# Transfers given to SyncE in a written order, and float64 conversions tied behind softmax steps, in an attention and two-stage mixture kernel

## The chip, the cores and the metric

The kernel runs on one core of one Trainium2 chip. The metric is device time in microseconds (us) of one execution of the whole program. Lower is better. TensorE (PE in the rows) multiplies and transposes, VectorE (DVE), ScalarE (ACT) and GpSimd (POOL) work on tiles, and SyncE (SP) gives transfers to the core's DMA engines: its queue takes them one after another, and a transfer whose condition isn't met yet holds back all that stand behind it.

## The reference

Three stages follow each other. Attention over 4 x 12 heads of 448 tokens and 64 features, with normalised queries and keys; a gated layer of 768 -> 1536 -> 768 on its 1792 output rows; and a mixture of 8 experts, of which each row takes one.

```python
q_n, k_n = rmsnorm(q, g_q), rmsnorm(k, g_k)
scores = scale * q_n @ k_n.T                       # 448 x 448 for each of 48 heads
attn = softmax(scores)
x = (attn @ v).reshape(1792, 768)
gate = 1 / (1 + exp(-(x @ w_gate)))
x = (gate * (x @ w_val)) @ w_out                   # moe_: 768 -> 1536 -> 768
e_idx = argmax(x @ w_gate2)                        # moe2_: one of 8 experts for each row
out[rows of e] = gate_w * eom * (relu(x @ w1[e]) @ w2[e])
```

## The kernel before

**Attention** runs in 24 pairs of heads, each in 8 slots, 192 slots in all. `attn_slot(n)` writes the scores of slot n+1 on TensorE (lines 364 and 365), the softmax step of slot n on VectorE (line 377: scale by the row and column factors and take the maximum; line 380 negates it) and ScalarE (line 381: exp with the sum), the four transposes of slot n-2 (line 410), and each fourth slot the product with the values (`av`, line 431). Three things go round through memory. The factors of the keys of a pair are copied by VectorE as a small tile `rk` (line 322), written to `rkd` (line 323) and read back broadcast to `rb` (line 324), which line 377 reads. The sums of a pair are copied as `rr` (line 393), written to `rsd` (line 394), and read back twice as `rs` (line 397); `features` multiplies by it (line 438, `xr`), after which the bank of `av` is free. And tokens `tok` (line 233) are squared on GpSimd (line 271) and summed on VectorE (line 272, into `sa`) for the Newton steps of `inv_root` (lines 289 to 292; its work tiles `sa` and `sw` come from the pool `sw`). `qk` (line 251) and `v` (line 241) are the other loads of a pair.

**The gated layer** runs over two halves of the rows, `moe1_steps(0)` and `moe1_steps(1)`: 48 products `up` (line 555, 18 matmuls each) and six rounds of `down` (line 578). Half 0 needs the first 12 pairs alone, and is woven into the slots from slot 101 on; half 1 begins when attention has ended. In half 0 each of 36 weight pieces comes as float64 (`kind == "wide"` in `piece_in`), in two parts: line 93 loads a part to `w` (two buffers), ScalarE (line 99) and VectorE (lines 101, 103, 105) turn it to float32 in `raw`, line 108 writes it to `wf` for half 1, and `piece_split` (lines 121 and 123) makes the two tiles `whi`, `wlo` that the matmuls read. `want(n)` calls for pieces some steps ahead. Half 1 reads `wf` back (line 111) and loads its features `e` from `xs` (line 874), split by lines 877 and 878. **The experts** come last, and draw on the same functions for their weights.

**What sets the order.** The program is traced in the order of the code, and a scheduler, which has a model of each instruction's time, then orders the instructions of every engine by when the model has them ready. That holds for SyncE's transfers as for arithmetic: a load may be moved ahead of slots, and a conversion between the steps of a softmax. A run-time wait can't change it: each engine takes its instructions as they stand. `tc.issue_after(ins)` ties what is traced under it behind `ins` on that engine's queue, without a wait for its end.

Of the kernel before, what the change touches and what calls it, by code (L numbers as in the profile page):

```python
# [38 lines left out]
PREP = "s1 t2", "K1", "s2", "K2", "", "", "t4", ""  # L39
PAIRED = 64  # L40
# [4 lines left out]
def attn_moe_moe_kernel(ctx, tc, qk, tokqk, tokv, g, wup, wout, wr, w1, w2, out):  # L45
# [34 lines left out]

    def add(key, kind, src, lead=False):
        index[key] = len(pieces)
        pieces.append((kind, src, lead))

    def piece_in(n):
# [4 lines left out]
        if kind == "wide":  # L90
            for c in range(0, DM, DM // PARTS):
                d = mp["w64"].tile([128, DM // PARTS, 2], I32, tag="w64", name="w64")
                last_in[0] = nc.sync.dma_start(
                    out=d, in_=src[:, 2 * c:2 * (c + DM // PARTS)].rearrange("p (c w) -> p c w", w=2))
# [12 lines left out]
            if not lead:  # L107
                nc.sync.dma_start(out=wf[n][:, LG:WO], in_=t[:, LG:WO])
        elif kind == "again":
            c = 0 if lead else LG  # L110
            nc.sync.dma_start(out=t[:, c:], in_=wf[src][:, c:])
        else:
            nc.sync.dma_start(out=t[:, LG:WO], in_=src())
# [82 lines left out]
    lot("sw", 1, 0)  # L196
# [29 lines left out]
    def load_tok(p):  # L226
# [4 lines left out]
        for i in range(0, 16, 8 if p == 0 else 16):  # L231
            i2 = i + 8 if p == 0 else 16
            nc.sync.dma_start(out=t[:, 16 - i2:16 - i], in_=tokqk[b, pr, :, 16 - i2:16 - i])
        tk_t[p] = t

    def load_v(p):
# [4 lines left out]
        nc.sync.dma_start(out=v_, in_=tokv[b, pr])  # L241
        v_t[p] = v_

    def load_qk(p):
# [4 lines left out]
        for h in halves(p):  # L249
            for i in range(2):  # L250
                nc.sync.dma_start(out=t[64 * i:64 * i + 64, :, h], in_=qk[b, pr, :, :, h])
        qk_t[p] = t

    def sums_sq(p):
# [18 lines left out]
        if p > 0:  # L273
            load_tok(p + 1)
# [28 lines left out]
    def krow(p):  # L303
# [4 lines left out]
        if p in DIRECT:  # L308
# [59 lines left out]
    def soft_max(n):  # L368
# [8 lines left out]
        nc.vector.tensor_tensor_reduce(  # L377
# [3 lines left out]
        nc.scalar.activation(  # L381
# [3 lines left out]
    def sums(p):  # L385
# [8 lines left out]
        nc.sync.dma_start(out=rsd[p], in_=rr)  # L394
        t = tile_of("rs", [128, S], F32, "rs")
        for h in range(2):
            nc.sync.dma_start(
                out=t[64 * h:64 * h + 64],
                in_=rsd[p:p + 1, 4 * h:4 * h + 4].rearrange("o c q -> o (c q)").to_broadcast([64, S]))
        rs_t[p] = t  # L400

# [33 lines left out]
    def features(p):  # L435
# [9 lines left out]
        else:  # L445
            nc.sync.dma_start(out=xs[b - 2, pr], in_=t)
# [3 lines left out]
    def stats(p):  # L450
        while did["t"] < p:
            did["t"] += 1
            sums_sq(did["t"])
# [6 lines left out]
    def splits(p):  # L460
        while did["s"] < p:
# [3 lines left out]
            loads(did["s"] + (2 if did["s"] < NPAIR // 2 - 3 else 1))  # L465
# [14 lines left out]
    def attn_slot(n):  # L480
# [7 lines left out]
        if i == 4 and n > 8:  # L488
# [699 lines left out]
```

## Time and profile before

| | us |
|---|---|
| median of 3 runs (lowest, highest) | 1287.24 (1284.73, 1288.29) |
| the profiled execution, its own time | 1288.62 |
| span of that execution, first to last instruction | 1286.8 |
| TensorE busy in it | 1185.8 (92%) |
| VectorE busy | 722.1 (56%) |
| ScalarE busy | 577.1 (45%) |
| GpSimd busy | 382.4 (30%) |

The span falls into stages. Up to 196 us there is attention alone; from 196 to 627 us slots and half 0 are woven; up to 686 us half 0 ends; up to about 952 us half 1; then the experts. A group of rows gives the busy time of each engine in each of these stretches. "Idle before" in a row is the time that the engine stood still just ahead of that instruction, with what ended it. The matmul ends are modelled, and a wait for several things is put down to the one that came last.

### The profile page before, as it was taken

The page shows a single profiled execution, that of the slowest core. Times are in us where ns is not written, and L with a number is a line of the kernel's source. Part 1 is how long each engine was busy: PE and PEld are TensorE (multiplying, and loading weights), DVE is VectorE, ACT ScalarE, POOL GpSimd, SP SyncE. Part 2 cuts the span into 40 slices and gives each one's busy share as a digit, 9 for nine tenths or more (in the row PEclk, how much of TensorE's full clock was granted, in tenths as well). Part 3 has the DMA queues.
Part 4 walks back from the last instruction along what each step waited for, and adds up shares of the span by engine and source line. Part 5 has one row for each costly group of instructions (what it writes and reads, how often), then busy time and mean ns, then how long its engine had stood idle before and what let it go on. Part 6 is the DMA issues. An engine that isn't in the chain of part 4 may idle for free.

```text
span 1286.8 us, 19940 instructions
## 1 busy us (share of the span) xinstructions
PE 1185.8 (92%) x7089; PEld 1039.4 (81%) x7089; DVE 722.1 (56%) x1709; ACT 577.1 (45%) x1174; POOL 382.4 (30%) x318
## 2 busy tenths in 40 slices
PE   5888888999999898997989999999969999999996
PEld 3665657677778787786879999999959998999996
DVE  7877878877568585775754224433454323333342
ACT  4656755556455353543441331122114434555553
POOL 3555645413132031310232000000023434545453
PEclk9888889899999999998999999999998999999999
DMA  9476666656536279476444121121037355566671
GB/s 219 128 181 172 153 163 201 186 144 184 146 96 196 88 199 234 132 197 151 150 139 136 50 63 50 42 71 50 13 123 273 114 194 186 190 207 222 209 269 43
DMA packets 77054, 191.92 MB, mean 149 GB/s; under 512 B 10617, under 2 KB 27513, under 8 KB 76944
## 3 DMA queue, kind: packets, MB, share of 16 engines
q1 hardware_dynamic: 74496, 179.52, 47.8%
q0 software_dynamic: 2448, 11.03, 2.3%
q8 instruction: 58, 0.95, 0.3%
q14 instruction: 52, 0.43, 0.1%
HBM read 154.43 MB, written 36.81 MB: 149 GB/s over the span
## 4 chain that ended last, share of the span: by engine, by line
PE 50%; DMA 2%; DVE 1%; issue 1%; SPq 0%; POOL 0%; ACT 0%; POOLq 0%; DVEq 0%
PE m L555 16%; PE d L1006 10%; PE m L578 9%; PE u L961 7%; PE d L961 3%; PE d L990 2%; DMA w<-in_wup_dram 1%; PE a L431 1%; PE u L940 1%; DMA raw<-in_w_dram 0%; DMA xg<-acc,slot 0%; PE t L410 0%; DMA g<-xg 0%; PE d L998 0%; PE m L597 0%
## 5 line engine op out<-in xcount | busy, mean ns | idle before, releaser
L121 ACT ACTIVATE whi<-raw 128x768 fp32r<-128x768 f32 (+1 forms) x200 | 167.1, 846 | 283.0 <-PE m L555 57.7
L123 POOL TENSOR_TENSOR wlo<-raw,whi 128x768 fp32r<-128x768 f32 (+1 forms) x100 | 188.9, 1896 | 311.4 <-ACT whi L121 268.4
L555 PE MATMUL m<-xh,whi 128*128 128x448 f32 x576 | 215.1, 374 | 4.5 <-DVE tanh L567 3.1
L555 PE MATMUL m<-xl,whi 128*128 128x448 f32 x576 | 212.4, 369 | 0.0
L555 PE MATMUL m<-xh,wlo 128*128 128x448 f32 x576 | 211.1, 367 | 0.0
L123 DVE TENSOR_TENSOR wlo<-raw,whi 128x768 fp32r<-128x768 f32 (+1 forms) x100 | 99.9, 1003 | 187.8 <-ACT whi L121 187.1
L381 ACT ACTIVATE e<-e,m 112x448 f32<-112x448 f32 x192 | 127.4, 665 | 89.8 <-DVE m L380 80.8
L377 DVE CUSTOM_DVE_ANT_0 e<-s,rb,sy 112x448 f32<-112x448 f32 x192 | 127.5, 672 | 32.2 <-PE s L365 17.6
L555 PEld LDWEIGHTS m<-xh,whi 128*128 128x128 f32 x576 | 109.6, 190 | 16.4 <-DVE tanh L567 3.3
L578 PE MATMUL m<-whi,hhi 128*128 128x392 f32 (+1 forms) x336 | 116.7, 352 | 4.5 <-DVE acc L584 2.7
L364 PE MATMUL s<-K,Q 128*112 128x448 f32 x192 | 87.1, 453 | 34.7 <-DVE m L377 24.5
L410 PE MATMUL t<-ident,e 112*112 112x112 f32 x768 | 109.9, 271 | 9.3 <-ACT et L418 6.4
L555 PEld LDWEIGHTS m<-xl,whi 128*128 128x128 f32 x576 | 109.4, 190 | 9.6 <-issue 1.7
L578 PE MATMUL m<-wlo,hhi 128*128 128x392 f32 (+1 forms) x336 | 115.4, 343 | 1.4 <-POOL wlo L123 1.4
L431 PE MATMUL a<-et,v 112*64 112x224 f32 x768 | 109.5, 379 | 7.7 <-ACT et L418 3.8
L410 PEld LDWEIGHTS t<-ident,e 112*112 112x112 f32 x768 | 87.6, 139 | 35.5 <-ACT et L418 8.8
L555 PEld LDWEIGHTS m<-xh,wlo 128*128 128x128 f32 x576 | 109.0, 189 | 8.6
L578 PE MATMUL m<-whi,hlo 128*128 128x392 f32 (+1 forms) x336 | 114.7, 341 | 0.0
L334 POOL TENSOR_TENSOR Q<-qk,Q 64x896 fp32r<-64x896 f32 (+1 forms) x25 | 56.0, 2240 | 172.4 <-DVE Q L333 93.5
L418 ACT ACTIVATE et<-t 112x448 f32<-112x448 f32 x168 | 87.1, 536 | 28.6 <-PE t L410 28.3
L584 DVE TENSOR_TENSOR acc<-m,acc 128x392 f32<-128x392 f32 (+1 forms) x140 | 77.2, 557 | 33.3 <-PE m L578 32.0
L733 POOL DMA_INDIRECT xg<-acc,slot x14 | 14.4, 1028 | 271.0 <-DVE slot L710 267.4
(209 smaller groups left out, 2399.2 us busy)
## 6 DMA issues: line engine op xcount, KB each, us to landing
raw<-in_w_dram SPq DMA_DIRECT2D x128, 384.0 KB
qk<-in_qk_dram SPq DMA_DIRECT2D x46, 448.0 KB
w<-in_wup_dram SPq DMA_DIRECT2D x48, 384.0 KB
tok<-in_tokqk_dram SPq DMA_DIRECT2D x23, 448.0 KB
wf<-raw SPq DMA_DIRECT2D x24, 384.0 KB
w<-in_wout_dram SPq DMA_DIRECT2D x24, 384.0 KB
raw<-wf SPq DMA_DIRECT2D x24, 384.0 KB
rb<-rkd SPq DMA_DIRECT2D x21, 392.0 KB
```

Source lines behind the costliest of these rows:

```text
L121: nc.scalar.activation(out=hi[:, c:], in_=t[:, c:], func=ACTF.Copy)
L123: eng.tensor_tensor(out=lo[:, c:], in0=t[:, c:], in1=hi[:, c:], op=ALU.subtract)
L364: nc.tensor.matmul(ps, lhsT=lhs, rhs=K1_t[p][:, h, :], start=True, stop=False)
L377: nc.vector.tensor_tensor_reduce(out=e, in0=ps, in1=rb_t[p][:, h, :], scale=r_t[p][:, i:i + 1], scalar=-3.0e38, op0=ALU.mult, op1=ALU.max, ...
L381: nc.scalar.activation(out=e, in_=e, func=ACTF.Exp, scale=1.0, bias=m[:, 1:2], accum_out=sum_t[p % 3][:, i, 0:1])
L410: nc.tensor.transpose(ps[0:CH, kc, :], e[:, kc * CH:(kc + 1) * CH], ident[0:CH, 0:CH])
L418: nc.scalar.activation(out=dst, in_=ps[0:CH], func=ACTF.Copy)
L431: nc.tensor.matmul(ps[64 * h:64 * h + 64, hf * 2 * CH:(hf + 1) * 2 * CH], lhsT=v_t[p][:, h, kc, :], rhs=ets[h][:, kc, :], start=(kc == 0), ...
L555: nc.tensor.matmul(ps[:, 0:S], lhsT=a, rhs=x, start=(n == 0), stop=(n == 3 * KD - 1))
L578: nc.tensor.matmul(ps[:, 0:c1 - c0], lhsT=l, rhs=r, start=(i == 0), stop=(i == 5))
L961: nc.tensor.matmul(ps[:, 0:c], lhsT=a, rhs=x[:, k, 0:c], start=(n == 0), stop=(n == 3 * KD - 1))
L1006: nc.tensor.matmul(ps[i, n][0:rows, 0:384], lhsT=l, rhs=s[:, c0:c0 + 384], start=(f == 0 and q == 0), stop=(f == NF2 - 1 and q == 2))
```

## The change

Eight edits, all of which move work and none of which removes an instruction: each engine has as many instructions of each kind as before.

- **A chain on SyncE.** `sp()` issues a transfer tied behind the last one that `sp()` issued. All transfers of attention and of half 0, the loads of `wf` in half 1 and those of `e` go through it, so that SyncE's order is that of the calls. Expert weights and gathers don't.
- **A clock in the code.** `passed(dt)` moves a counter: 1.9 for each slot behind the first pair, and the planner's cost of each step of the gated layer. `later(dt, fn)` puts a call off until the counter has gone dt further. `WAITS` holds four such distances: 1.5 for the small writes (`rkd`, `rsd`, `xs`, the last `wf`), 5.5 for the read-backs `rb` and `rs`, 6.0 for `qk` and `tok`, 5.0 for the `wf` write of a converted piece and the load of the next one.
- **Conversions behind softmax.** The four conversion instructions of each part are tied behind the softmax instructions of the last slot traced, on VectorE (line 377) and ScalarE (line 381).
- **Loads apart from conversions.** `wide_load(n)` loads both parts of a piece, and is called for piece n+1 once piece n has been converted.
- The pool `sw` of `inv_root` gets two buffers in place of one.
- `features` is traced at slot 5 of the next pair in place of 4.
- The first pieces are called for one by one (slots 96, 98 and 100 in place of all at slot 96), and the first `up` is traced at slot 102 in place of 101.
- The zero rows of `xg` stand in the chain in place of behind the last weight load.

```diff
@@ -78,9 +80,55 @@
+    def later(dt, fn):
+        due.append((clock[0] + dt, fn))
+
+    def passed(dt):
+        clock[0] += dt
+        while True:
+            ready = [x for x in due if x[0] <= clock[0]]
...
+            x = min(ready, key=lambda x: x[0])
+            due.remove(x)
+            x[1]()
...
+    def sp(out, in_):
...
+            with tc.issue_after(last_sp[0].ins):
+                last_sp[0] = nc.sync.dma_start(out=out, in_=in_)
...
+    def wide_load(n):
...
+        for c in range(0, DM, DM // PARTS):
+            d = mp["w64"].tile([128, DM // PARTS, 2], I32, tag="w64", name="w64")
+            last_in[0] = sp(
...
+            wide_t[n].append((c, d))
...
     def piece_in(n):
...
         if kind == "wide":
...
+            wide_load(n)
+            after = ExitStack()
+            for x in last_slot.values():
+                after.enter_context(tc.issue_after(x.ins))
+            for c, d in wide_t.pop(n):
...
-            if not lead:
-                nc.sync.dma_start(out=wf[n][:, LG:WO], in_=t[:, LG:WO])
+            after.close()
+
+            def transfers():
+                if not lead:
+                    sp(out=wf[n][:, LG:WO], in_=t[:, LG:WO])
+                wide_load(n + 1)
+
+            later(WAITS[3], transfers)
...
-    lot("sw", 1, 0)
+    lot("sw", 2, 0)
...
-            load_tok(p + 1)
+            if last and clock[0]:
+                later(WAITS[2], lambda: load_tok(p + 1))
+            else:
+                load_tok(p + 1)
...
-        nc.sync.dma_start(out=rkd[p], in_=rr)
-        nc.sync.dma_start(
-            out=t, in_=rkd[p:p + 1].rearrange("o (h c) q -> o h (c q)", h=2).to_broadcast([CH, 2, S]))
+        later(WAITS[0], lambda: sp(out=rkd[p], in_=rr))
+        later(WAITS[1], lambda: sp(
+            out=t, in_=rkd[p:p + 1].rearrange("o (h c) q -> o h (c q)", h=2).to_broadcast([CH, 2, S])))
...
-        nc.sync.dma_start(out=rsd[p], in_=rr)
+        later(WAITS[0], lambda: sp(out=rsd[p], in_=rr))
...
+        later(WAITS[1], back)
...
-            loads(did["s"] + (2 if did["s"] < NPAIR // 2 - 3 else 1))
+            to = did["s"] + (2 if did["s"] < NPAIR // 2 - 3 else 1)
+            if clock[0]:
+                later(WAITS[2], lambda: loads(to))
+            else:
+                loads(to)
...
-        if i == 4 and n > 8:
+        if i == 5 and n > 8:
             features(p - 1)
...
+        passed(1.9 if p > 0 else 0.0)
...
             open_moe()
+            want(0, 0, 0)
+        if n == NSLOT // 2 + 2:
+            want(0, 0, 1)
+        if n == NSLOT // 2 + 4:
             want(0, 1, 2)
...
         fn()
+        passed(c)
```

On SyncE, in attention alone, before (`rkd`, `rb`: write and read-back of the keys' factors; `rsd`, `rs`: of the sums; numbers tell the tiles of one pair from those of the next):

```order
L323 DMA rkd_68<-rk_555 8x112
L233 DMA tok_745<-in_tokqk_dram 112x1024
L324 DMA rb_552<-rkd_68 112x896
L251 DMA qk_899<-in_qk_dram 64x1792
L394 DMA rsd_69<-rr_691 8x112
L251 DMA qk_899<-in_qk_dram 64x1792
L241 DMA v_985<-in_tokv_dram 112x512
L397 DMA rs_694<-rsd_69 64x448 x2
L323 DMA rkd_68<-rk_750 8x112
```

and in the changed kernel, at the same pairs (its line 108 is the one in `sp()`):

```order
L108 DMA rsd_69<-rr_691 8x112
L108 DMA tok_718<-in_tokqk_dram 112x1024
L108 DMA rkd_68<-rk_743 8x112
L108 DMA rs_693<-rsd_69 64x448 x2
L108 DMA qk_785<-in_qk_dram 64x1792 x2
L108 DMA rb_740<-rkd_68 112x896
L108 DMA v_804<-in_tokv_dram 112x512
L108 DMA tok_806<-in_tokqk_dram 112x1024
L108 DMA rsd_69<-rr_886 8x112
```

Most pairs of this stretch now have the same row of transfers: both small writes, `rs`, `qk`, `rb`, `v`, `tok`. Before, `rb` stood right behind its write and one `tok`, and ahead of `qk`.

On SyncE, where slots and half 0 are woven, before (the sums of one pair; `w64` is the load of a part of a piece, `w` in the profile):

```order
L394 DMA rsd_69<-rr_4395 8x112
L397 DMA rs_4398<-rsd_69 64x448 x2
L93 DMA w64_4307<-in_wup_dram 128x768
L323 DMA rkd_68<-rk_4472 8x112
L108 DMA wf_70<-raw_4241 128x768
L93 DMA w64_4313<-in_wup_dram 128x768
L324 DMA rb_4469<-rkd_68 112x896
```

and in the changed kernel, the sums of the same pair:

```order
L108 DMA wf_70<-raw_4267 128x768
L108 DMA w64_4315<-in_wup_dram 128x768
L108 DMA w64_4317<-in_wup_dram 128x768
L108 DMA w64_4341<-in_wup_dram 128x768
L108 DMA w64_4343<-in_wup_dram 128x768
L108 DMA rsd_69<-rr_4377 8x112
L108 DMA wf_70<-raw_4324 128x768
L108 DMA wf_70<-raw_4340 128x768
L108 DMA w64_4445<-in_wout_dram 128x768
L108 DMA w64_4447<-in_wout_dram 128x768
L108 DMA rkd_68<-rk_4441 8x112
L108 DMA rs_4379<-rsd_69 64x448 x2
```

The write of the sums and that of the keys' factors now stand behind loads and write-backs of pieces, with the read-backs together behind them.

On TensorE, at the first `up` (`m` is its bank), before:

```order
L391 MATMUL t<-ident,sum 8x112
L410 MATMUL t<-ident,e 112x112 x4
L320 MATMUL t<-ident,sy 8x112
L431 MATMUL a<-et,v 64x224 x16
L364 MATMUL s<-K_2122,Q 112x448
L365 MATMUL s<-K_2123,Q 112x448
L555 MATMUL m<-xh,whi 128x448
L555 MATMUL m<-xl,whi 128x448
```

and in the changed kernel:

```order
L472 MATMUL t<-ident,e 112x112 x4
L493 MATMUL a<-et,v 64x224 x7
L472 MATMUL t<-ident,e 112x112 x8
L422 MATMUL s<-K_2309,Q 112x448
L423 MATMUL s<-K_2310,Q 112x448
L622 MATMUL m<-xh,whi 128x448
L622 MATMUL m<-xl,whi 128x448
```

Before, 91 scores stand ahead of the first `up`; now there are 103.

## Rows read from the trace of the kernel before

**Rows 1.** Windows: us, busy time (instructions) of PE, PEld, DVE, ACT, POOL; clock; DMA; GB/s.

```profile
10.00:50.00 40.00, 29.27 (x141) 21.58 (x141) 32.41 (x86) 19.36 (x41) 18.05 (x16) 0.91 0.84 196
50.00:196.00 146.00, 121.25 (x816) 86.77 (x816) 114.99 (x345) 97.06 (x240) 81.80 (x96) 0.90 0.63 163
196.00:300.00 104.00, 98.09 (x552) 77.24 (x553) 84.39 (x203) 59.68 (x134) 44.59 (x44) 0.96 0.58 170
300.00:627.00 327.00, 304.41 (x1752) 256.24 (x1749) 224.09 (x546) 157.54 (x342) 69.00 (x45) 0.97 0.59 162
627.00:686.00 59.00, 54.46 (x310) 46.81 (x309) 39.09 (x88) 20.15 (x40) 13.60 (x10) 0.97 0.38 122
686.00:952.00 266.00, 266.00 (x1383) 251.06 (x1382) 102.43 (x180) 62.00 (x100) 9.20 (x10) 1.00 0.19 59
952.00:1287.00 335.00, 311.86 (x2147) 299.45 (x2145) 119.25 (x241) 158.53 (x279) 143.62 (x88) 0.97 0.57 193
```

**Rows 2.** Waits of VectorE, 40 to 300 us: total us, times, longest us.

```profile
DVE e L377 <- DMA rb<-rkd: 10.8, 5, 4.5
...
DVE sa L272 <- POOL sw L290: 6.8, 4, 3.0
DVE xr L438 <- DMA rs<-rsd: 6.1, 5, 2.9
```

**Rows 3.** Waits of TensorE, 40 to 196 us.

```profile
PE s L364 <- DVE m L377: 14.8, 10, 4.2
...
PE a L431 <- DVE xr L438: 2.9, 3, 2.3
```

**Rows 4.** Timeline of SyncE, 57 to 76 us: start, us, transfer, how many.

```profile
63.10 0.43 SPq L323 DMA_DIRECT2D rkd<-rk  x1
63.62 0.33 SPq L233 DMA_DIRECT2D tok<-in_tokqk_dram  x1
69.03 0.31 SPq L324 DMA_DIRECT2D rb<-rkd  x1
```

**Rows 5.** Timeline of VectorE at four moments; idle time before it in brackets.

```profile
72.37 0.68 DVE L377 CUSTOM_DVE_ANT_0 e<-s,rb,sy 112x448 f32<-112x448 f32 x1 [4.47 <-DMA rb<-rkd]
...
114.94 0.62 DVE L438 TENSOR_TENSOR xr<-a,rs 128x448 f32<-128x448 f32 x1 [2.92 <-DMA rs<-rsd]
...
336.81 0.36 DVE L101 TENSOR_SCALAR w<-w 128x384 int32<-128x384 int32 x1 [2.98 <-DMA w<-in_wup_dram]
...
592.82 0.36 DVE L101 TENSOR_SCALAR w<-w 128x384 int32<-128x384 int32 x1 [2.86 <-DMA w<-in_wup_dram]
```

**Rows 6.** Timeline of TensorE at five moments.

```profile
73.12 0.71 PE L364 MATMUL s<-K,Q 128*112 128x448 f32 x1 [4.16 <-DVE m L377]
...
115.62 0.60 PE L431 MATMUL a<-et,v 112*64 112x224 f32 x4 [2.33 <-DVE xr L438]
...
194.94 0.67 PE L364 MATMUL s<-K,Q 128*112 128x448 f32 x1 [2.10 <-DVE m L377]
...
338.26 1.31 PE L431 MATMUL a<-et,v 112*64 112x224 f32 x6 [1.87 <-ACT et L418]
...
593.83 0.42 PE L522 MATMUL m<-tlo,wrs 128*32 128x256 f32 x1 [3.31 <-DVE tlo L514]
```

**Rows 7.** Waits of SyncE, 40 to 300 us.

```profile
SPq L233 <- DVE sa L272: 21.9, 7, 13.0
```

**Rows 8.** Waits of VectorE, 300 to 627 us.

```profile
DVE w L101 <- DMA w<-in_wup_dram: 34.3, 19, 5.3
DVE w L101 <- DMA w<-in_wout_dram: 22.8, 11, 4.3
```

**Rows 9.** Groups of VectorE, 50 to 196 us: count, busy us, mean ns, idle before.

```profile
L377 DVE CUSTOM_DVE_ANT_0 e<-s,rb,sy 112x448 f32<-112x448 f32 x77 | 50.8, 670 | 15.9 <-DMA rb<-rkd 10.8 <-PE s L365 5.0
```

**Rows 10.** Timeline of SyncE where half 0 ends.

```profile
654.95 4.84 SPq L874 DMA_DIRECT2D e<-xs  x5
...
663.20 1.14 SPq L111 DMA_DIRECT2D raw<-wf  x2
```

More of the change, by code (lines that the diff above doesn't have):

```diff
@@ L250, in load_qk, with sums_sq @@
             for i in range(2):
-                nc.sync.dma_start(out=t[64 * i:64 * i + 64, :, h], in_=qk[b, pr, :, :, h])
+                sp(out=t[64 * i:64 * i + 64, :, h], in_=qk[b, pr, :, :, h])
         qk_t[p] = t
-    def sums_sq(p):
+    def sums_sq(p, last=False):
         if p >= NPAIR:
@@ L393, in sums, with back @@
         nc.vector.tensor_copy(out=rr, in_=ps[0:8, 0, :])
-        nc.sync.dma_start(out=rsd[p], in_=rr)
+        later(WAITS[0], lambda: sp(out=rsd[p], in_=rr))
         t = tile_of("rs", [128, S], F32, "rs")
[L396 to L399, printed above, removed]
         rs_t[p] = t
+        def back():
+            for h in range(2):
+                sp(
+                    out=t[64 * h:64 * h + 64],
+                    in_=rsd[p:p + 1, 4 * h:4 * h + 4].rearrange("o c q -> o (c q)").to_broadcast([64, S]))
+        later(WAITS[1], back)
     def transp(n):
@@ L445, in features @@
         else:
-            nc.sync.dma_start(out=xs[b - 2, pr], in_=t)
+            later(WAITS[0], lambda: sp(out=xs[b - 2, pr], in_=t))
     did = {"s": 0, "k": 0, "q": 1, "t": 0}
@@ L541, in lead_put @@
                 out=t[:, 0:LG], in0=ps[:, 32 * j + LG:32 * j + 2 * LG], in1=t[:, 0:LG], op=ALU.add)
-            nc.sync.dma_start(out=wf[n], in_=t)
+            later(WAITS[0], lambda n=n, t=t: sp(out=wf[n], in_=t))
             led.add(n)
@@ L813, in zero_rows @@
             rows = xg[e * NT + r:e * NT + r + n, :]
[L814 to L815 removed]
+            sp(out=rows[:, 0:2 + DM // 4], in_=zrow[0:n])
+            sp(
                 out=rows[:, 2 + DM // 4:].rearrange("p (a c) -> p a c", a=3),
@@ L853, in attn_moe_moe_kernel @@
     first = n
-    left = NSLOT + 5 - first
+    left = NSLOT + 6 - first
     spent = 0.0
@@ L858, in attn_moe_moe_kernel @@
         fn()
+        passed(c)
         spent += c
         while zeroed < NE and spent > total * (0.6 + 0.04 * zeroed):
-            with tc.issue_after(last_in[0].ins):
-                zero_rows(zeroed)
+            zero_rows(zeroed)
             zeroed += 1
-        while n < NSLOT + 5 and (n - first) < left * spent / total:
+        while n < NSLOT + 6 and (n - first) < left * spent / total:
             attn_slot(n)
             n += 1
-    while n < NSLOT + 5:
+    while n < NSLOT + 6:
         attn_slot(n)
         n += 1
+    passed(100.0)
     for tg in range(2):
```

45 lines of the change are left out of this document (29 added, 16 removed).

## The prediction

> **What bounds the kernel now.** I read the stages first [rows 1]. From 686 us to 952 us TensorE is never idle, and from 952 us on the order of all engines is the same in the changed kernel, so whatever the change does to the time it does before 686 us. There TensorE stands still for 24.8 us of attention alone (146.00 less 121.25), 5.9 us up to 300 us, 22.6 us up to 627 us and 4.5 us up to 686 us, and the first 50 us hold some 20 us of start. That is the purse: about 58 us behind the start, of which some belongs to arithmetic.
>
> Attention alone has no single bound: TensorE is busy for 0.83 of it and VectorE for 0.79, at a granted clock of 0.90 of the 2.4 GHz level, and each waits for the other in turn. So a stop of VectorE is a stop of TensorE a moment later. VectorE stops there for memory: 10.8 us for the read-back `rb`, 6.1 us for `rs`, 6.8 us for the Newton work tile [rows 2]. TensorE's waits in the same stretch are mostly for line 377 [rows 3]. The largest pair shows the chain. SyncE writes `rkd` at 63.10 us, gives out a `tok`, and can issue `rb` at 69.03 us alone, when the write has landed [rows 4]. VectorE's next softmax step begins at 72.37 us after 4.47 us of nothing [rows 5], and TensorE's scores at 73.12 us after 4.16 us [rows 6]. Six gaps of TensorE come right behind such a stop, from the one at 73.12 us to the one at 194.94 us, together 13.6 us.
>
> In the woven stage VectorE stops for 57.1 us for weight loads [rows 8]. TensorE has other work there, so less of it shows: six gaps, from 338.26 us to 593.83 us, 14.7 us together, follow such a stop [rows 5, 6].
>
> **The change, part by part.** The sum is made against the profiled execution's 1288.62 us, which is 1.4 us above the median of 1287.24 us.
>
> *Read-backs and the Newton tile in attention alone.* The second buffer of `sw` removes a wait by name: the sum of squares no longer waits for the Newton steps of the group before, which are the 6.8 us. For `rs` I counted in the order the VectorE work between the copy `rr` and the product that needs `rs`, each instruction at its group's mean, as the softmax step at 670 ns [rows 9]. It was 5 to 8 us for the first 12 pairs and is 5 to 17 us in the changed kernel, since `features` is traced a slot later: that wait should nearly go. For `rb` the count from `rk` to the first softmax step of its pair doesn't grow as a whole. The three tightest are 4.4, 5.2 and 6.0 us of VectorE work, 5.6, 6.6 and 7.6 us at its share of 0.79. What must fit in there is the write, its landing, the issue of `rs` and `qk` and the landing of `rb`. The worst chain of before took 9.3 us from write to step (63.10 to 72.37), and at that price the three are short by 3.7, 2.7 and 1.7 us, 8.1 us in all. If everything fits, nothing is left over. I take 3 us, nearer to the lower end, since the worst chain had a `tok` between the write and the read-back and the new one has not. So of 13.6 us some 10.6 us go: **-10.6 us, between -5.5 and -13.6**.
>
> *The start.* The chain puts the tokens of pair 2 behind the `qk` of pair 3, and the Newton steps of pairs 1 and 2 need them. In this stretch the DMA engines are busy for 0.84 at 196 GB/s [rows 1], so 448 KB more ahead of a load is 2.3 us. `tok` of later pairs then also comes later, and the order has two of their sums ahead of the last Newton step. Some of that is hidden by the softmax steps of pair 0, whose followers get their `qk` earlier by the same edit. **+1 us, 0 to +3.**
>
> *The first `up` 12 slots later.* TensorE's work is the same, but 12 slots of it lose their filler. A slot takes 1.9 us in attention alone (77 softmax steps in 146 us [rows 9]); idle is 0.17 of attention alone and 0.06 from 196 to 300 us [rows 1]. 12 x 1.9 x 0.11 = 2.5 us. **+2.5 us, +1 to +4**, the upper end if VectorE's conversions crowd into what follows.
>
> *Weight loads in the woven stage.* A load can begin when the conversion of two parts before has ended. I counted the VectorE work between that end and the first conversion instruction of the new part: 46 of 70 had under 4 us before, 35 of 70 now, and the time short of 4 us falls by a quarter (65 to 49 us). The loads of a `down` round stay tight, with 1 to 2 us each in both kernels. A quarter of the 14.7 us of TensorE is **-3.5 us**. For the ends: all of it, -14.7, or as much again, if the distance of 5.0 behind a conversion makes loads late that were early. Here the trace speaks for SyncE's patience: in 40 to 300 us it stood 21.9 us for token buffers that VectorE still read [rows 7], so a load given out earlier would only have stood at the head of the queue.
>
> The Trainium skill's page "DMA: Bandwidth & Descriptors", section "Rules for kernel authors", says the opposite of this edit: to issue a transfer early, compute, and wait late. By that rule the distances of 5.0 and 6.0 would cost something wherever the buffer was free already. The waits of SyncE just named show that often it was not. What that rule would give is the third rival below.
>
> *Small writes behind weight loads.* In the woven stage the chain has a price that is not there before. The write of the sums stands behind loads whose buffers VectorE frees later than it makes the sums: by the count, up to 14 us of VectorE work, for nine of the last 12 pairs, and the write of the keys' factors by up to 18 us. The scheduler has put the readers back too: what remains from the delayed write to the product is 3.4 to 14 us of VectorE work, at the share of 0.69 in this stage 5 to 20 us. Between issue of a write and a landed read-back lie 5.8 to 9.3 us in the rows of attention alone [rows 4, 5]. One or two pairs come up short by up to 4 us. Queued behind the waiting product are the softmax steps and conversions, and TensorE's next `av` waits for its bank. **+1 us, 0 to +6.**
>
> *The end of half 0.* Before, five of the 12 loads of `e` went out at 654.95 us, ahead of the `wf` loads at 663.20 us [rows 10]. Now all 12 stand behind those. The last products of half 0 run until 686 us, and the first half of the `e` tiles is needed then; 12 loads of 224 KB at 170 GB/s are 16 us. It fits, with VectorE's splits among the additions that TensorE waits for. **+1 us, 0 to +6.**
>
> The write-backs, the zero rows and the tie of the conversions itself I cost at nothing: SyncE has time, and the same conversions run on the same engines. What hides the tie is the filler of TensorE. If that runs out, it is in the gaps just counted.
>
> Sum: -10.6 + 1 + 2.5 - 3.5 + 1 + 1 = -8.6 us, 1280.0 us against the profiled execution, and 1278.6 us against the median.
>
> **The rivals.** *The waits go in the woven stage too.* If all of the 14.7 us go rather than a quarter, and nothing is left over of `rb`, it is another 14 us: 1264 us. For it: the tie keeps a conversion whose load hasn't landed from standing ahead of softmax steps. Against it: the tight loads in the `down` rounds.
>
> *A new bound in place of the old.* TensorE is busy for 0.83 of attention alone. If the six gaps only turn into other short waits between VectorE and TensorE, the first term shrinks to its lower end of 5.5 us, the second and third take 3 of it back, and the weight loads stay as they were: 1284 to 1290 us, no change to be told.
>
> *Slower: the chain holds the sums.* One mechanism, in the woven stage: a write of `rsd` or `rkd` waits behind a load for which VectorE has yet to convert, VectorE itself waits for the read-back, and so the conversion that would free the queue comes later still. It decides from the point where the chain of 9.3 us doesn't fit between the delayed write and its reader. If each of the nine delayed pairs pays what the worst read-back cost before, 4.16 us of TensorE, that is 37 us; with half of it covered by products 19 us, and with the first three terms kept (-7.1) it gives 1299 us. For it: the counts of 14 and 18 us. Against it: the readers were moved too.
>
> *Slower: loads come late.* By the rule above, as a mechanism of this kernel: each of 36 pieces waits on VectorE once more as long as the mean of now (57.1 us over 30 waits, 1.9 us). That is 68 us of VectorE, and at the present ratio of TensorE's gaps to VectorE's stops there (14.7 to 57.1) 18 us: 1287 + 18 - 7 = 1298 us.
>
> **How the numbers follow.** About 0.3%, 4 us, can be told from no change. The forecast, 1272 to 1283 us, has a chance of 0.48; the larger gain 0.16; no change 0.17; the chain holding the sums 0.14; late loads 0.05. So faster 0.64, same 0.17, slower 0.19. The likeliest time is 1278.6 us. The range of 8 in 10 reaches from 1262 us, the larger gain with its bounds, to 1293 us, through the case of no change and the milder part of the slower ones.
>
> **What would show it.** In the profile after: VectorE's waits for `rb`, `rs` and the Newton tile in 40 to 300 us, 23.7 us now, at 3 to 8 us; TensorE idle in attention alone about 0.1 of the stretch rather than 0.17; pair 1 beginning no earlier than now; the first `up` at some 205 to 215 us, not 196 us, with 12 slots more behind it; VectorE's waits for weight loads at 40 to 50 us rather than 57.1; half 1 beginning at about 677 us. I am wrong if VectorE waits for `rs` or `rb` in the woven stage by more than a few us, if its waits for weight loads grow, or if TensorE's idle time in attention alone stays though the named waits are gone.

## The result, and the profile after

The changed kernel is slower by 1.2%: 1301.80 us median (1296.91 to 1303.31, 4 runs) against 1285.99 us of the kernel before (4 runs), a ratio of 1.0116, 95% interval 1.0083 to 1.0149. The prediction was 1278.6 us, 1262 to 1293. Its profiled execution took 1303.31 us, with a span of 1301.2 us.

The windows of the changed kernel, by its own stages, with the columns of [rows 1]: attention alone now ends at 227 us, the last slot is at 640 us, half 1 begins at 700.4 us.

```profile
10.00:50.00 40.00, 25.57 (x119) 18.29 (x119) 29.53 (x77) 15.50 (x34) 16.06 (x19) 0.93 0.79 170
50.00:227.00 177.00, 146.44 (x940) 104.25 (x940) 134.00 (x393) 111.93 (x279) 81.83 (x94) 0.85 0.53 135
227.00:300.00 73.00, 65.53 (x377) 55.03 (x375) 55.32 (x137) 40.26 (x88) 24.46 (x23) 0.95 0.67 197
300.00:640.00 340.00, 315.36 (x1812) 267.85 (x1811) 226.88 (x567) 164.03 (x351) 86.25 (x62) 0.96 0.58 164
640.00:700.40 60.40, 56.13 (x322) 47.57 (x320) 36.73 (x84) 21.27 (x39) 10.28 (x7) 1.00 0.41 124
700.40:966.00 265.60, 265.55 (x1378) 250.66 (x1379) 105.80 (x188) 62.70 (x102) 12.53 (x13) 1.00 0.20 62
```

Half 1 begins 14.4 us later than before (700.4 to 686.0) and from there to the end both take the same 600.8 us, so the whole loss lies ahead of it, as the prediction said any difference would. TensorE's idle time ahead of half 1 grew from 78.1 to 90.7 us, its busy time by 1.7 us. The stages of that idle time, before and after: first 50 us 20.3 and 23.8; to the first `up` 24.8 and 30.6; to 300 us 5.9 and 7.5; to the last slot 22.6 and 24.6; to half 1 4.5 and 4.3.

The waits of VectorE, 40 to 300 us, changed kernel (in total, times, longest):

```profile
DVE Q L391 <- DMA qk<-in_qk_dram: 20.1, 8, 4.2
DVE e L435 <- PE s L423: 9.1, 10, 2.5
DVE w L150 <- DMA w<-in_wup_dram: 6.6, 5, 2.7
DVE xr L500 <- DMA rs<-rsd: 4.4, 7, 1.3
DVE sa L327 <- POOL tok L326: 4.1, 2, 2.3
```

The waits that the change was to remove are gone: of [rows 2], 23.7 us, there are 4.4 us for `rs` left and 0.8 us for `rb`. In their place stand 20.1 us for `qk`, which line 391 turns to `Q`. The timelines of SyncE, VectorE and TensorE show how that comes about (start, us, transfer or instruction; idle time before it in brackets):

```profile
77.54 0.28 SPq L108 DMA_DIRECT2D rsd<-rr  x1
94.29 0.28 SPq L108 DMA_DIRECT2D rkd<-rk  x1
94.66 1.09 SPq L108 DMA_DIRECT2D rs<-rsd  x2
95.88 1.15 SPq L108 DMA_DIRECT2D qk<-in_qk_dram  x2
```
```profile
67.29 1.31 DVE L403 SCALAR_TENSOR_TENSOR K<-qk,gg,K 128x896 fp32r<-128x896 f32 x1
...
94.00 0.26 DVE L380 COPY rk<-k 8x112 f32<-8x112 f32 x1 [0.17 <-PE k L378]
...
102.40 0.63 DVE L391 CAST Q<-qk 128x896 fp32r<-128x896 f32 x1 [3.26 <-DMA qk<-in_qk_dram]
```
```profile
106.94 0.71 PE L422 MATMUL s<-K,Q 128*112 128x448 f32 x1 [4.23 <-DVE m L435]
```

In this stage `qk` has two buffers, which the pairs take in turn. The load at 95.88 us is that of pair 7 (the first pair is 0), and its buffer is that of pair 5, which VectorE read for the last time until 68.60 us (the row of line 403). So it went out 27.3 us after its buffer was free, because it stood in the chain behind `rsd` and then `rkd`, whose 8x112 values VectorE made only at 94.00 us. SyncE had been standing since 77.54 us. The load then landed after VectorE had run out of work, VectorE stopped for 3.26 us, TensorE for 4.23 us. Some 4 us earlier it would have been in time. That is the rule here and no single case: the loads of pairs 6 to 12 went out 12 to 37 us after their buffers were free, and 0.0 to 2.9 us after in the kernel before, whose VectorE waited for none of these seven. The same row of four transfers comes again: `rkd` at 139.66 us, 8 us after `rsd`, and then

```profile
148.59 0.63 DVE L391 CAST Q<-qk 128x896 fp32r<-128x896 f32 x1 [4.05 <-DMA qk<-in_qk_dram]
```
```profile
153.13 0.71 PE L422 MATMUL s<-K,Q 128*112 128x448 f32 x1 [5.21 <-DVE m L435]
```

and again at 196.59 us (4.21 us of VectorE). The waits of SyncE in 40 to 300 us, of the changed kernel and then the answering one of the kernel before:

```profile
SPq L108 <- DVE m L438: 53.8, 9, 16.5
SPq L108 <- DVE rr L451: 40.6, 5, 19.7
```
```profile
SPq L394 <- DVE rr L393: 19.1, 4, 6.5
```

Line 438 is put down for the first, since it ended right by the copy of `rk`; its longest, 16.5 us, is the one up to 94.29 us. SyncE's patience was what the prediction relied on, and here it is what costs.

### The profile page after: what moved, and what is told of

Same layout as the page of the kernel before. It is cut to its first block, busy times and chain, and to the rows that moved or that the text cites. A ratio compares the mean times of both kernels' runs of the same rounds, so it can differ in the third digit from the quotient of the medians.

```text
span 1301.2 us, 19891 instructions
## 1 busy us (share of the span) xinstructions
PE 1186.9 (91%) x7089; PEld 1043.3 (80%) x7089; DVE 714.4 (55%) x1709; ACT 577.6 (44%) x1174; POOL 378.1 (29%) x318
## 4 chain that ended last, share of the span: by engine, by line
PE 44%; DMA 2%; DVE 2%; issue 1%; SPq 1%; ACT 1%; POOL 0%; POOLq 0%; DVEq 0%; ACTq 0%
PE m L622 14%; PE d L1079 9%; PE u L1034 7%; PE m L645 7%; PE d L1034 3%; PE d L1063 2%; PE u L1013 1%; DMA raw<-in_w_dram 0%; DMA e<-xs 0%; DMA g<-xg 0%; DMA w<-in_wout_dram 0%; DVE acc L651 0%; ACT whi L176 0%; SPq L977 0%; PE d L1071 0%
## 5 line engine op out<-in xcount | busy, mean ns | idle before, releaser
L493 PEld LDWEIGHTS a<-et,v 112*64 112x64 f32 x768 | 60.4, 147 | 44.7 <-issue 7.6
```

Of the source, the lines that this page charges most:

```text
L493: nc.tensor.matmul(ps[64 * h:64 * h + 64, hf * 2 * CH:(hf + 1) * 2 * CH], lhsT=v_t[p][:, h, kc, :], rhs=ets[h][:, kc, :], start=(kc == 0), ...
```

## The experiments

Each run has its own runs of the kernel before on the same chip (medians 1280.2 to 1286.7 us), so ratios are compared. One execution's profile can lie some us from the median of its kernel. Kernels without a chain have the zero rows behind the last weight load, as before.

**Taking transfers out of the chain.** First `qk` alone (its two lines as before, the rest of the change kept):

```diff
-                sp(out=t[64 * i:64 * i + 64, :, h], in_=qk[b, pr, :, :, h])
+                nc.sync.dma_start(out=t[64 * i:64 * i + 64, :, h], in_=qk[b, pr, :, :, h])
-                later(WAITS[2], lambda: loads(to))
+                loads(to)
```

> The changed kernel with one edit: the loads of qk stand outside the chain on SyncE and are traced right behind the splits, as before, so that the scheduler places them. Theory (the chain makes a load whose buffer is free wait behind small writes whose values VectorE has not made yet; the queries' cast then waits for its load: 20.1 us in 40 to 300 us in the changed kernel, 1.4 us before): these waits fall below 6 us and the time to 1283 to 1292 us. Rival one (the first up 12 slots later is what costs): the time stays above 1297 us, since here too 103 scores stand ahead of it. Rival two (the late start of pair 1 by 3.6 us runs through): a gain of no more than 4 us, 1297 us or more unless pair 1 starts earlier too.

1291.38 us, ratio 1.0029 (1.0003 to 1.0056). VectorE's waits for `qk` from the start to the first `up` fell from 17.0 to 2.3 us, and three quarters of the loss went with them. In 40 to 300 us other waits came up: 15.1 us for `tok`, still in the chain (4.1 us in the changed kernel), 10.8 us for `rb` and 9.5 us for `rs`.

The other way to the same end is `qk` within the chain, but sooner:

```diff
-                later(WAITS[2], lambda: loads(to))
+                later(2.0, lambda: loads(to))
```

> The changed kernel with one number changed: the loads of qk are put off by 2.0 in place of 6.0 and so stand in the chain behind the write of the sums but ahead of the write of the keys' factors, its read-back and rs. The chain stays whole. Theory: the casts' waits for qk fall from 20.1 us to under 10 us, and the time to 1285 to 1295 us; what is left is the wait behind the write of the sums. Rival one and two: 1297 us or more.

1302.57 us, ratio 1.0131 (1.0100 to 1.0161): the number was missed. The wait went over to `tok` (16.8 us of VectorE's sums waiting for squares, and 11.6 us for `qk`). So it isn't the place of one load in the row.

`qk`, `tok` and `v` out of the chain, traced as before; and, apart from that, the four small transfers out of the chain and the loads in it:

```diff
-            sp(out=t[:, 16 - i2:16 - i], in_=tokqk[b, pr, :, 16 - i2:16 - i])
+            nc.sync.dma_start(out=t[:, 16 - i2:16 - i], in_=tokqk[b, pr, :, 16 - i2:16 - i])
...
-        sp(out=v_, in_=tokv[b, pr])
+        nc.sync.dma_start(out=v_, in_=tokv[b, pr])
```
```diff
-        later(WAITS[0], lambda: sp(out=rkd[p], in_=rr))
+        later(WAITS[0], lambda: nc.sync.dma_start(out=rkd[p], in_=rr))
...
-        later(WAITS[0], lambda: sp(out=rsd[p], in_=rr))
+        later(WAITS[0], lambda: nc.sync.dma_start(out=rsd[p], in_=rr))
```

> The changed kernel with the loads of qk, tok and v outside the chain and traced where they were before; small writes, read-backs and weight transfers stay in it. In the second run the wait only moved from qk to the next load in the chain (tokens, 16.8 us). Theory (loads whose buffers are free wait behind small writes): with all three kinds of load free, VectorE's waits for qk and for the squared tokens in attention alone are under 8 us together, and the time is 1277 to 1288 us. Rival (any order fixed by hand costs, since small writes also hold small writes and weights): waits for rb and rs of over 15 us take their place, 1290 us or more.

> The other half: small writes rsd and rkd and the read-backs rs and rb outside the chain (still put off by 1.5 and 5.5 in the code); loads and weight transfers stay in it and stand behind each other alone. Theory: the small writes are what holds the chain, 1276 to 1288 us, waits for qk and tokens under 8 us together in attention alone. Rival (loads hold loads, because a qk or token load stands behind one whose buffer VectorE still reads): 1293 us or more, with those waits near 20 us.

1279.95 us, 0.9948 (0.9928 to 0.9968), and 1286.11 us, 0.9996 (0.9977 to 1.0016). The loads out of the queue bring all of the loss back, the small transfers out of it three quarters, which is what a queue does in which each holds up the other. In the second, VectorE's waits for `qk` and `tok` in attention alone were forecast at under 8 us and came to 12.9 us, so loads also held up loads. In the first, SyncE gives out between 77 and 97 us what the changed kernel gave out only from 94 us on:

```profile
77.65 0.28 SPq L108 DMA_DIRECT2D rkd<-rk  x1
...
85.24 0.27 SPq L108 DMA_DIRECT2D rkd<-rk  x1
...
88.97 1.11 SPq L306 DMA_DIRECT2D qk<-in_qk_dram  x2
```

Both sides out, so that only weights, write-backs, `xs`, `e` and zero rows stand in the chain; and no chain at all (`sp()` issues without the tie):

```diff
-            with tc.issue_after(last_sp[0].ins):
-                last_sp[0] = nc.sync.dma_start(out=out, in_=in_)
+            last_sp[0] = nc.sync.dma_start(out=out, in_=in_)
```

> The changed kernel with qk, tok, v and all four small transfers (rkd, rsd, rs, rb) outside the chain, so that only weight loads, their write-backs, zero rows, xs and e stand in it; the tie and the late weight loads stay. Theory (the loss is loads behind small writes, either half of it enough to bring it back): the loss is there once and can't be won back twice, 1276 to 1284 us, no more than 4 us below the kernel with free loads (1279.95). Rival (the chain of the weights has a price of its own in the woven stage): 1285 to 1292 us, with TensorE idle for over 17 us from 300 us to the last slot, against 11.9 us without any chain.

> The changed kernel with all edits but the chain: the transfers are traced where they are now, but not tied to each other (the zero rows behind the last weight load, as before). Theory: VectorE's waits for qk are gone, the second buffer of the Newton pool and the later features keep their gain, and the time is 1270 to 1287 us. Rival one (102 scores ahead of the first up): 1295 us or more.

1279.28 us, 0.9947 (0.9926 to 0.9969), and 1279.88 us, 0.9958 (0.9931 to 0.9984). The chain of the weights costs nothing; TensorE's idle time from 300 us to the last slot is 9.5 us with it, 11.9 us without, 22.6 us before. So the chain's whole price, 1.6% or 20 us, is in the transfers of attention.

Then the loads inside the chain as early as the code calls them, and the chain alone on the calls of the kernel before:

```diff
-                later(WAITS[2], lambda: loads(to))
+                loads(to)
...
-                later(WAITS[2], lambda: load_tok(p + 1))
+                load_tok(p + 1)
```

> The changed kernel with qk and tok not put off by 6.0 but given to the chain where the code calls them, which is ahead of the pair's small writes. Theory (any one order in which these stand in one queue pays, since now the small writes stand behind loads whose buffers are not free, or tok behind qk): 1290 to 1302 us. Rival (only the distance of 6.0 was wrong, and issue early is enough within the chain): 1277 to 1286 us, like the kernel with free loads (1279.95).

> The chain alone, on the calls as they stood before: no distances, no tie, loads with their conversions, one buffer of sw, features at slot 4, the slots' lead as before. Each pair's transfers then stand as rsd, rs, qk, tok, rkd, rb, v, so that every read-back stands right behind its write and holds what is behind it until the write has landed. Theory (the loss is of one fixed order of transfers that wait for different things): 1296 to 1320 us, SyncE standing for rsd and rkd to land and qk and tok late. Rival (the distances made the loss): 1284 to 1292 us.

1299.26 us, 1.0107 (1.0072 to 1.0142), and 1354.89 us, 1.0581 (1.0535 to 1.0627), which is more than expected. Early is not enough within the one order: in the first SyncE waits about as long as in the changed kernel, in the second also for its own small writes to land, which the read-back right behind each must await:

```profile
SPq L108 <- DVE m L435: 47.1, 8, 15.9
SPq L108 <- DVE rr L448: 45.5, 4, 20.3
```
```profile
SPq L108 <- DMA rkd<-rk: 57.6, 12, 7.0
```

The other edits thus gave back 4.6 of the 5.8% that the chain costs on the calls of before. The Trainium skill's page "DMA: Bandwidth & Descriptors", section "Rules for kernel authors", tells to issue early and wait late; the runs agree with it only where the early transfer has nothing unfinished ahead of it.

**The tie.** Taken out of the changed kernel; put alone into the kernel before; and taken out together with the chain:

```diff
-                after.enter_context(tc.issue_after(x.ins))
+                pass
```

> The changed kernel without the tie of the conversions behind the last slot's softmax steps; the chain is whole. Theory: the tie is not what costs, 1297 to 1305 us, and VectorE's waits for qk stay near 20 us. Rival (the tie delays weights that TensorE waits for): 1294 us or less, with less idle time of TensorE behind the first up.

> The kernel before with one edit: the conversions tied behind the softmax steps of the last slot traced. Without the chain 102 scores then stand ahead of the first up, not 91. If the first up 12 slots later costs, as I put it in the sum, with nothing gained: 1288 to 1292 us. If the tie is what made the woven stage better in the run without the chain (TensorE idle 11.9 us there, 22.6 us before): 1277 to 1284 us.

> The changed kernel without the chain and without the tie: what is left are the second buffer of the Newton pool, features a slot later, the weight loads split from their conversions and traced later, and the put-off transfers. 91 scores stand ahead of the first up. If the tie carries the gain of the run without the chain: 1283 to 1290 us, with VectorE's waits for weight loads back above 60 us in the woven stage. If the other edits carry it: 1276 to 1282 us.

1306.23 us, 1.0149 (1.0122 to 1.0176); 1288.23 us, 1.0018 (0.9996 to 1.0039); 1290.99 us, 1.0031 (1.0009 to 1.0053). The tie is not the loss, and alone it gains nothing. But without the chain it is worth 0.7% (1.0031 to 0.9958). In the last of the three VectorE's waits for weight loads were 53.6 us, not over 60 us, as forecast if the tie carries the gain.

**The edits to attention.** The largest wait of [rows 2] by itself: the kernel before, whose `rb` is loaded from a row of the input, so that no softmax step can wait for a read-back. It leaves out the right factors, so its rows go to other experts.

```diff
-            out=t, in_=rkd[p:p + 1].rearrange("o (h c) q -> o h (c q)", h=2).to_broadcast([CH, 2, S]))
+            out=t, in_=qk[0, 0, 0:1, :, 0].to_broadcast([CH, 2, S]))
```

> The kernel before, with rb loaded from a row of the input qk in place of the keys' factors read back from rkd; so the softmax works with other factors, and the rows go to other experts: only the time up to the start of half 1 (686.0 us before) is compared. No softmax step can then wait for a read-back. This measures the largest part of the prediction's first term by itself (10.8 us of VectorE's waits, five of the six gaps of TensorE). If the prediction had that term right, half 1 starts at 675 to 679 us and TensorE's idle time from 50 us to the first up falls from 24.8 us to 14 to 17 us. Rival: VectorE and TensorE wait for each other anyway, and the named wait passes to another name: half 1 at 682 to 688 us, idle time 21 to 25 us.

Half 1 began at 670.5 us in the profile, earlier than either theory had it, but that was its fastest execution (1271.79 us; the median of 8 is 1275.52 us). By the ratio, 0.9949 (0.9920 to 0.9978), 6.5 us go, of which up to 1.4 us can be the other experts' (599.4 us from half 1 on in its profile, 600.8 us before). TensorE's idle time from 50 us to the first `up` stayed at 25.2 us, as the rival said; what shrank in this profile is that from 300 us to the last slot, 14.9 us after 22.6 us, and the busy time up to half 1, by 6.9 us. VectorE's wait went over to `rs`:

```profile
DVE xr L438 <- DMA rs<-rsd: 14.8, 5, 5.4
```

The woven stage's edits without those of attention (no chain; distances of the small transfers, `qk` and `tok` zero, one buffer of `sw`, `features` at slot 4), and the reverse, the edits to attention alone (no chain, no tie, loads with their conversions):

```diff
-    lot("sw", 2, 0)
+    lot("sw", 1, 0)
-        if i == 5 and n > 8:
+        if i == 4 and n > 8:
```
```diff
-                wide_load(n + 1)
-
-            later(WAITS[3], transfers)
+            transfers()
```

> The kernel without a chain (1279.88) with its edits to attention taken back too: one buffer of sw, features at slot 4, rkd, rb, rsd, rs, qk and tok traced at once, and the slots' lead as before. What is left of the change are the tie, the loads apart from the conversions, and the late write-backs. Theory now (the gain without a chain lies in the woven stage, and the edits to attention are worth nothing): 1277 to 1284 us. If the prediction's -10.6 us for attention were there behind the chain's loss: 1287 to 1292 us. If the edits to attention cost time: 1270 to 1276 us.

> The edits to attention alone: no chain, no tie, loads with their conversions and write-backs as before; what is left is the second buffer of sw, features a slot later, and the small writes, read-backs, qk and tok traced later by 1.5 to 6.0. The first up has 91 scores ahead of it, as before. If the prediction's term for attention alone stands by itself: 1274 to 1280 us. Rival (the edits to attention gain only where the tie keeps conversions out of the softmax steps): 1284 to 1291 us, with TensorE idle for 22 to 28 us from 50 us to the first up.

1285.18 us, 1.0006 (0.9985 to 1.0028), which lies between the two theories, and 1290.35 us, 1.0076 (1.0056 to 1.0096), the rival's or, by the ratio, more. The term of -10.6 us is not there by itself; its edits cost 10 us.

**The second buffer of `sw`.** One buffer again, in four companies: no chain, the edits to attention alone, weights alone in the chain, and the changed kernel.

```diff
-    lot("sw", 2, 0)
+    lot("sw", 1, 0)
```

> The kernel without a chain (1279.88) with one buffer of sw again. If the second buffer is worth its part of the prediction's first term (6.8 us of VectorE's waits, of which at most some 4 us are TensorE's): 1283 to 1287 us, with waits of the sum for the Newton tile back at 4 us or more. Rival (the wait only changes its name): 1278 to 1282 us.

> The edits to attention alone (1.0076 of before) with one buffer of sw: what is left is features a slot later and the small writes, read-backs, qk and tok traced later. If the second buffer costs some 0.5%: 1.001 to 1.004. Rival (the distances themselves cost where the tie is absent): 1.006 to 1.010.

> The kernel with weight loads alone in the chain (0.9947 of before) with one buffer of sw. If the second buffer costs some 0.5%: 0.988 to 0.992. Rival (the difference seen without a chain was the order of that one kernel): 0.993 to 0.997.

> The changed kernel with one buffer of sw. If the second buffer costs by itself (some 0.5%): 1.005 to 1.009 of before, against 1.0116. Rival (in the chain it makes no difference, since the loads behind the small writes set the time): 1.010 to 1.014. If it is a gain, as predicted: 1.015 to 1.018.

| company | two buffers | one buffer |
|---|---|---|
| no chain | 0.9958 (0.9931 to 0.9984) | 0.9912 (0.9885 to 0.9939), 1271.16 us |
| edits to attention alone | 1.0076 (1.0056 to 1.0096) | 0.9975 (0.9942 to 1.0007), 1283.06 us |
| weights alone in the chain | 0.9947 (0.9926 to 0.9969) | 0.9884 (0.9815 to 0.9954), 1271.69 us |
| changed kernel | 1.0116 (1.0083 to 1.0149) | 1.0101 (1.0035 to 1.0167), 1301.21 us |

In the second line the intervals stand apart; in the first and third they overlap at the ends, and all point the same way. In the changed kernel nothing can be told. A gain, as predicted, it is nowhere. The runs of the first two lines with one buffer came out faster than either forecast for them. Groups of VectorE, 50 to 196 us, of the kernel with weights alone in the chain (columns of [rows 9]), first with two buffers:

```profile
L327 DVE TENSOR_REDUCE sa<-tok 112x16 f32<-112x1024 f32 x17 | 20.4, 1205 | 4.8 <-POOL tok L326 2.6 <-POOL sw L345 2.1
L400 DVE SCALAR_TENSOR_TENSOR K<-qk,gg,K 128x896 fp32r<-128x896 f32 x10 | 17.2, 1718 | 0.2 <-ACT K L399 0.2
...
L388 DVE CAST Q<-qk 128x896 fp32r<-128x896 f32 x10 | 9.2, 924 | 2.1 <-DMA qk<-in_qk_dram 2.1
```

then with one:

```profile
L327 DVE TENSOR_REDUCE sa<-tok 112x16 f32<-112x1024 f32 x15 | 17.7, 1207 | 9.0 <-POOL tok L326 9.0
L400 DVE SCALAR_TENSOR_TENSOR K<-qk,gg,K 128x896 fp32r<-128x896 f32 x10 | 13.7, 1372 | 0.0
...
L388 DVE CAST Q<-qk 128x896 fp32r<-128x896 f32 x10 | 6.9, 692 | 0.0
```

With two buffers the scheduler takes the sums of later groups sooner: of 25 sums, 20 lie ahead of 140 us in place of 15, and 58 softmax steps in place of 67 (without a chain 20 and 15 sums, 64 and 67 steps). So sums that are not needed yet stand ahead of softmax steps, on an engine that is busy for 0.8 of this stretch. And the same instructions take longer: `K` and `Q` together 26.4 us against 20.6 us, 10 of each. More on that at the end.

Where the time went, the rows of TensorE show. Up to half 1, with the columns of [rows 1], the same two kernels, two buffers and then one:

```profile
0.00:678.60 678.60, 607.17 (x3563) 487.08 (x3564) 491.06 (x1281) 358.38 (x794) 220.46 (x219) 0.95 0.59 163
0.00:668.30 668.30, 599.91 (x3564) 484.51 (x3564) 485.65 (x1281) 356.54 (x795) 222.62 (x219) 0.96 0.60 165
```

Of the 10.3 us, 3.0 us are idle time and 7.3 us are busy time, for the same work at a higher granted clock. In stretches granted 0.5, the 1.2 GHz level, TensorE was busy for 58.4 us with two buffers and for 44.4 us with one; half of that difference is 7.0 us. In the first two lines of the table its busy time is shorter by 6.5 us too, while its idle time is 5.1 and 9.9 us longer (in both lines the profiled execution with two buffers is the fastest of its kernel). Over all executions the mean granted clock is 0.968 and 0.974 in the first line, 0.965 and 0.970 in the second, 0.967 and 0.975 in the third, 0.957 and 0.959 in the last. By the ratios the second buffer costs 6, 13 and 8 us in the first three lines; some 7 us in each are time of TensorE at the lower level. That the early sums bring that about is argued; no run shows it.

The kernels with one buffer, without a chain or with weights alone in it, beat the kernel before and the changed one.

## Why the prediction was wrong

**The purse was right, and so was the tail.** All of the difference lies ahead of half 1, and the time behind it did not move.

**The step that failed first** is the chain's price. "Small writes behind weight loads" counted the writes behind work of VectorE, in the woven stage alone, and found +1 us. There it was right: VectorE's waits for `rs` and `rb` from 300 to 640 us are 2.8 and 0.6 us, and the chain of weights costs nothing. (The 5.8 us of that term stand in none of the rows it names: they have 5.93 us from the write to the issue of the read-back, and 9.27 us to the step that reads it.) But the step left out what the chain does in attention alone, and so put it at nothing there: the same count was never made for the loads that stand behind those writes, nor for this stage, whose row of transfers (`rsd`, `tok`, `rkd`, `rs`, `qk`) stood in the order printed ahead of the prediction. The argument from [rows 7], that a load given out earlier would only have stood at the head of the queue, was taken from `tok`. For `qk` SyncE stood too before (12.6 us in 40 to 300 us, for line 345 and for GpSimd's line 334), but there such a load went out within 2.9 us of its buffer's being free. In the chain it stood behind writes that wait for something else. The measured price is 20 us (1.0116 to 0.9958), far outside the term's bounds of 0 to +6. The rival "the chain holds the sums" had the mechanism, a write that waits for VectorE in an ordered queue, but the wrong stage and the wrong victim. "Loads come late" had the victim's kind, but weights in place of `qk` and `tok`; its 1298 us came near for another reason.

**Read-backs and the Newton tile, -10.6 us.** The named waits went, as predicted (23.7 to 5.2 us), and TensorE's idle time in attention alone did not (0.17 of the stretch in both), which the prediction named as the sign that it was wrong. Nor did the distances remove the wait for `rb` by themselves: with `qk` in time it is back, 10.8 us with `qk` alone out of the chain, 9.5 us with no chain, 11.0 us with weights alone in it. In the changed kernel VectorE waited for `qk` instead. Each stop of VectorE was priced as a stop of TensorE that disappears with it. The run without any read-back of the keys' factors shows what the largest wait held: 6.5 us (3 to 10) of the whole run and, in its profile, nothing of TensorE's idle time in attention alone, with `rs` next in line. The Newton tile's 6.8 us are those of 40 to 300 us, 3.8 us of them ahead of 196 us, and the second buffer that removes them had the wrong sign: where the loads were in time it cost 0.5 to 1.0%. The edits alone cost 10 us in place of giving 10.6 us; without that buffer they give 3 us, with an interval that reaches past none.

**The start, +1 us, 0 to +3.** Pair 1 began at 48.0 us, not 44.4 us, and TensorE's idle time in the first 50 us grew by 3.5 us, just outside. Without a chain it begins at 44.5 us, with one buffer besides at 42.1 us.

**The first `up` later, +2.5 us.** The kernel before with the tie alone has 102 scores ahead of it and is at 1.0018, 2.3 us, which fits, though its interval holds none too and the run has the tie as well. At 226.9 us it came later than the 205 to 215 us given, since the slots themselves were late.

**Weight loads, -3.5 us.** VectorE's waits for them over 300 to 640 us, against 57.1 us before [rows 8]:

```profile
DVE w L150 <- DMA w<-in_wup_dram: 26.1, 15, 6.8
...
DVE w L150 <- DMA w<-in_wout_dram: 18.8, 8, 4.1
...
DVE Q L391 <- DMA qk<-in_qk_dram: 8.6, 4, 4.1
```

44.9 us, within the 40 to 50 us forecast. TensorE got nothing of it in the changed kernel (idle 24.6 us, 22.6 us before), since `qk` and `tok` were late here too, by 8.6 and 8.8 us. With no chain, or weights alone in it, its idle time there is 7.6 to 13.5 us: this term was sized too small. It needs the tie and the edits to attention together: without the one it is 18.2 us (1.0031 of before), without the others 15.6 us (1.0006). Why neither gains alone is not settled, and the late loads by themselves were not taken out.

**The end of half 0, +1 us.** From the last softmax step to half 1 it is 60.1 us, before 58.9 us, with the same idle time. Right.

What is left of the change without attention in the chain and without the second buffer measures 0.988 to 0.991 of before, 11 to 15 us. So there was a gain of the size foretold, but not where it was foretold. With weights alone in the chain and one buffer, half 1 begins 17.7 us sooner than before in the profiles: the woven stage from 300 us to the last slot has 15.0 us less idle time, the rest up to half 1 has 5.3 us more, and TensorE's busy time is 8.0 us shorter, at a granted clock of 0.96 in place of 0.95, which the sum had no term for. The two edits that were counted at nothing and as a gain took more than this away.

## What to carry to other kernels

Before several streams of transfers are tied into one order, go through that order and ask of each one not only when its own condition is met, but what stands behind it whose buffer is already free: a 3.6 KB write that waits for a value holds up every load behind it. Weights, which nobody but one consumer waits for, could be chained here at no cost; small writes and loads of another stream could not, and moving the loads earlier in the chain did not help. And a second buffer that removes a wait by name can still cost time (0.5 to 1.0% here in three kernels, nothing to be told in the fourth): see whether the work that it lets loose is wanted yet, and compare TensorE's busy time and granted clock as well as its idle time.

## What had not been expected of the hardware

The same VectorE instruction took up to 3.7 times as long beside work of GpSimd. Timeline of VectorE, then of GpSimd, weights alone in the chain and two buffers:

```profile
104.02 2.25 DVE L388 CAST Q<-qk 128x896 fp32r<-128x896 f32 x1
107.04 2.52 DVE L400 SCALAR_TENSOR_TENSOR K<-qk,gg,K 128x896 fp32r<-128x896 f32 x1
...
133.18 0.61 DVE L388 CAST Q<-qk 128x896 fp32r<-128x896 f32 x1
133.78 1.13 DVE L400 SCALAR_TENSOR_TENSOR K<-qk,gg,K 128x896 fp32r<-128x896 f32 x1
```
```profile
103.89 1.89 POOL L326 TENSOR_TENSOR tok<-tok 112x1024 f32<-112x1024 f32 x1 [1.53 <-DMA tok<-in_tokqk_dram]
...
106.51 2.11 POOL L389 TENSOR_TENSOR Q<-qk,Q 64x896 fp32r<-64x896 f32 x1
```

At 104.02 us the square of the tokens had begun 0.13 us earlier, and the conversion ended 0.49 us after it, about the 0.61 us that it takes at 133.18 us, where GpSimd did no square. The Trainium skill's page "SBUF — State Buffer", section "Who interferes with whom", says that the two engines share a pair of ports and that, where instructions of both need it, the one that comes first holds it for its whole length while the other stands; these rows agree. Such lengthening (instructions of 40 to 200 us that took over 1.3 times the lower quartile of their group, and what they took beyond it) came to 11 to 15 us of VectorE in the first three lines of the table with two buffers, and to about 6 us with one. It doesn't decide the time by itself: the changed kernel has 13 us with two buffers and 8 us with one, with no difference in time to be told, and the kernel before, with one, has 10 us. What part of the second buffer's cost it makes is not shown.
